# Attention over a key-value cache on one core: the first K block loaded in two transfers, 16 partitions and then 112

## The chip, the core and the metric

The kernel runs on one core of a Trainium2 chip. Its time is the device time of one execution in microseconds. A core has five engines that run side by side, each with its own instruction list: TensorE (PE) for matrix products, VectorE (DVE), ScalarE (ACT), GpSimd (POOL) and SyncE (SP), which here does nothing but issue loads and one store. Loads are carried out by 16 DMA engines. On-chip memory has 128 partitions; a tile is so many partitions by so many bytes in each.

## The reference

Grouped-query attention with four new tokens for each of eight sequences, over a cache of 2048 keys: 32 query heads share 8 key-value heads.

```python
B, Sq, D = 8, 4, 512
Hq, Hkv, Sk, Dh = 32, 8, 2048, 128
q = (x @ wq).reshape(B, Sq, Hq, Dh).transpose(0, 2, 1, 3)
k = repeat(k_cache, Hq // Hkv, axis=1)
v = repeat(v_cache, Hq // Hkv, axis=1)
scores = einsum("bhqd,bhkd->bhqk", q, k) * Dh ** -0.5
p = softmax(scores)
o = einsum("bhqk,bhkd->bhqd", p, v)
out = o.transpose(0, 2, 1, 3).reshape(B, Sq, Hq * Dh) @ wo
```

All tensors are bf16. The two caches hold 33.5 MB each, wq and wo 4.2 MB each: about 75.5 MB must be read.

## The kernel before

The work is cut into 16 units; a unit `u` is four key-value heads of one sequence. Its keys are one tile of 128 partitions with 16 KB in each (2 MB): partition `g * 32 + s` holds 64 consecutive keys of head `g`. The 2 MB are one contiguous piece of the cache. `load_k(u)` loads the keys of a unit with one transfer (lines 88 to 91), `load_v(u)` the values (line 99). Three buffers each stand for K and V.

All loads are issued by SyncE on one queue, in an order written by hand: K0, then `wq_sb` (line 107, 4 MB), `x_sb` (line 108, 32 KB), K1, K2, V0; then K3, V1, K4, V2 and so on, and at last the four blocks of wo in six pieces (line 104). `load_ready` issues a load as soon as its buffer can be free in the program's order; on the chip the issue then waits until the buffer's last reader is done. The queue works through its transfers in the order of issue, 16 DMA engines side by side, and several transfers stand in it at any time.

The steps of a unit:

- `turn_keys` (line 137): VectorE turns the keys in two halves with 32 by 32 transposes, `kt` from `k_sb`. The first of them waits for the K load. When both are done, the K buffer is free and SP can issue the next K load into it.
- `scores` (line 215): TensorE multiplies queries (`q_bd`) and turned keys.
- `maxima`, `exponentials`, `probs_to_keys`: VectorE takes the maximum (line 233), ScalarE the exponential (line 251), VectorE turns the result (line 261), and ScalarE and GpSimd copy it to `probs` (line 271).
- `values` (line 300): TensorE multiplies with V, two units later.

Before unit 0's scores can run, the queries are made: x is turned (line 147, into `xT_sb`, line 150), multiplied with wq (line 157), scaled (lines 172 and 174), turned (line 181) and spread (line 193). All of this needs x, which stands in the queue behind K0 and wq. Unit 0's two transposes come first on VectorE, ahead of the copy of line 150.

At the end TensorE projects with wo (`project`, line 368), ScalarE copies `out_ps` (line 432) and two small stores write the output.

Of the kernel before, what the change touches and what calls it, by code (L numbers as in the profile page):

```python
# [8 lines left out]
BF16 = mybir.dt.bfloat16  # L9
# [5 lines left out]
def kernel(  # L15
# [9 lines left out]
    nc = tc.nc  # L25

    B, Sq, D = x.shape
    _, Hkv, Sk, Dh = k_cache.shape
# [5 lines left out]
    G = 4  # L34
    S = 128 // G
    C = Sk // S
# [18 lines left out]
    kpool = ctx.enter_context(tc.tile_pool(name="kpool", bufs=KB))  # L55
# [25 lines left out]
    units = [(hq, b) for hq in range(Hkv // G) for b in range(B)]  # L81
    ks = [None] * NU
    vs = [None] * NU

    def load_k(u):
        hq, b = units[u]
        ks[u] = kpool.tile([128, C, Dh], BF16, tag="k_sb", name="k_sb")
        nc.sync.dma_start(
            ks[u][:, :, :],
            k_cache[b, G * hq : G * hq + G].rearrange("g (s c) d -> (g s) c d", c=C),  # L90
        )
# [11 lines left out]
        w0 = p * WR + r0  # L103
        nc.sync.dma_start(wo_sb[:, w0 : w0 + n, :], rows[:, r0 : r0 + n, :])

    load_k(0)
    nc.sync.dma_start(wq_sb[:, :, :], wq.rearrange("(p r) n -> p r n", r=R))
    nc.sync.dma_start(x_sb[:, :], x.flatten_outer_dims())
    loads = [("k", 1)]
# [355 lines left out]
```

## Time and profile before

| | |
|---|---|
| three runs | 185.65, 190.73, 190.85 us; median 190.73 |
| the profiled execution | 185.65 us |
| its span, first to last instruction | 183.9 us |
| mean granted TensorE clock | 0.907 |
| busy: PE, DVE, ACT, POOL | 124.5, 119.3, 83.3, 57.2 us |
| read from memory | 75.53 MB, 411 GB/s over the span |
| issue to landing: K0, x, median of K loads | 7.9, 17.0, 20.3 us |

The profile is of one execution. Its page gives the busy time of each engine, then the span in 40 equal slices, where a digit is the busy share of a slice in tenths (9 is 90% or more); the DMA line is the mean over the 16 DMA engines. The chain of waits follows the work that ended last back to what released each step. Times in the timeline are microseconds from the start of the span, with the start first and the duration behind it; what stands in brackets is the idle time before an instruction and what ended it. "SPq" is an issue of a load on SyncE's queue: its duration is that of the issue and not of the transfer.

### The profile page before, as it was taken

Reading aid. Unit: us, or ns where it says so; the run is one execution under the profiler, and the core shown is the slowest. Engines: PE = TensorE matmul, PEld = TensorE weight load, DVE = VectorE, ACT = ScalarE, POOL = GpSimd, SP = SyncE. Lnnn points to the kernel's source line nnn. Section 1 sums busy time; section 2 is a strip of 40 time slices with the busy share of each in tenths; the row PEclk is TensorE's granted clock in tenths of the full one; section 3 lists DMA queues with packets and bytes.
Section 4 is the critical chain, followed back from the end, with each engine's and each line's share of the span. In section 5 each row is a group of like instructions: output and inputs, shape, how many; then the busy total and the mean of one; then the engine's idle time right before and its main releaser. Section 6 shows DMA issues by size and latency. Waiting matters only on the chain.

```text
span 183.9 us, 2569 instructions
## 1 busy us (share of the span) xinstructions
PE 124.5 (68%) x964; PEld 82.1 (45%) x964; DVE 119.3 (65%) x147; ACT 83.3 (45%) x154; POOL 57.2 (31%) x122
## 2 busy tenths in 40 slices
PE   0000465437959796887978858399867977499992
PEld 0000141202626574755736626247453746269770
DVE  0180234968597989989889777567857685936210
ACT  2000130272825674946847646346572638084020
POOL 8920000152405151632534515142332415056000
PEclk9999999655887999999999999958996699879999
DMA  6999999999999999999999999999999999999980
GB/s 185 471 435 389 442 417 446 417 442 428 424 442 417 446 413 437 421 435 431 428 431 428 438 413 438 438 428 435 417 442 417 442 421 435 438 411 429 421 366 19
DMA packets 5915, 75.71 MB, mean 412 GB/s; under 512 B 688, under 2 KB 784, under 8 KB 1296
## 3 DMA queue, kind: packets, MB, share of 16 engines
q1 hardware_dynamic: 5856, 75.55, 96.8%
q8 instruction: 7, 0.11, 0.2%
q14 instruction: 4, 0.03, 0.0%
q10 hardware_dynamic: 48, 0.02, 0.0%
HBM read 75.53 MB, written 0.03 MB: 411 GB/s over the span
## 4 chain that ended last, share of the span: by engine, by line
DMA 51%; DVE 30%; PE 14%; ACT 2%; issue 1%; SPq 0%; ACTq 0%; DVEq 0%
DMA k_sb<-in_k_cache_dram 24%; DVE kt L137 21%; DMA v_sb<-in_v_cache_dram 9%; DMA x_sb<-in_x_dram 9%; PE s_ps L215 9%; DMA wo_sb<-in_wo_dram 8%; DVE top L233 5%; PE o_ps L300 3%; DVE swapped L225 1%; DVE q_g L174 1%; PE psq L157 1%; DVE q_bd L193 1%; ACT q_g L172 1%; PE pse L181 1%; DVE less L239 1%
## 5 line engine op out<-in xcount | busy, mean ns | idle before, releaser
L137 DVE STREAM_TRANSPOSE kt<-k_sb 128x2048 f32<-128x2048 f32 x32 | 72.0, 2288 | 17.5 <-DMA k_sb<-in_k_cache_dram 17.4
L215 PE MATMUL s_ps<-kt,q_bd 128*64 128x512 bf16 x256 | 44.5, 479 | 33.1 <-DVE kt L137 33.1
L300 PE MATMUL o_ps<-v_sb,probs 128*128 128x256 bf16 x512 | 61.3, 281 | 0.0
L271 POOL COPY probs<-p_t 32x512 bf16<-32x512 bf16 x63 | 38.6, 612 | 59.4 <-DVE r_sb L289 57.1
L300 PEld LDWEIGHTS <-probs 128*128 128x128 bf16 x512 | 50.5, 101 | 12.1 <-issue 5.2
L271 ACT COPY probs<-p_t 32x512 bf16<-32x512 bf16 x62 | 38.1, 615 | 19.7 <-DVE r_sb L289 18.5
L215 PEld LDWEIGHTS <-q_bd 128*64 128x64 bf16 x256 | 17.3, 126 | 49.7 <-issue 25.2
L233 DVE TENSOR_REDUCE top<-s_ps 128x1 f32<-128x1024 f32 x16 | 19.6, 1224 | 16.7 <-PE s_ps L215 16.7
L251 ACT ACTIVATE s_sb<-s_ps,less 128x1024 bf16<-128x1024 f32 x16 | 22.4, 1400 | 9.8 <-DVE less L239 9.6
L225 POOL COPY l_swapped<-l_sb 64x1 f32<-64x1 f32 x32 | 5.8, 180 | 50.3 <-ACT s_sb L251 49.6
L324 ACT CAST oT<-o_t 128x64 bf16<-128x64 f32 x16 | 3.4, 212 | 33.3 <-PE o_t L323 33.3
L147 PE MATMUL xtp<-ident,x_sb 32*128 32x32 bf16 x4 | 0.3, 194 | 18.7 <-DMA x_sb<-in_x_dram 18.7
L316 ACT ACTIVATE o_sc<-o_ps,r_sb 64x128 f32<-64x128 f32 x28 | 10.1, 362 | 5.9 <-PE o_ps L300 5.7
L172 ACT ACTIVATE q_g<-psq 32x512 bf16<-32x512 f32 x4 | 2.4, 588 | 21.6 <-DVE q_g L174 21.6
L261 DVE STREAM_TRANSPOSE p_t<-s_sb 128x512 f32<-128x512 f32 x16 | 10.7, 672 | 1.6 <-ACT s_sb L251 1.6
L147 PEld LDWEIGHTS <-x_sb 32*128 32x128 bf16 x4 | 0.2, 114 | 18.7 <-DMA x_sb<-in_x_dram 18.7
L323 PEld LDWEIGHTS o_t<-both,o_sc 128*128 128x128 f32 x32 | 5.4, 211 | 7.1 <-issue 6.1
L323 PE MATMUL o_t<-both,o_sc 128*128 128x64 f32 x32 | 7.5, 320 | 0.2 <-DVE o_sc L318 0.2
L130 POOL MEMSET probs<- 128x4096 bf16 x2 | 7.0, 3511 | 0.0
L174 DVE TENSOR_SCALAR q_g<-psq 32x512 bf16<-32x512 f32 x4 | 2.7, 681 | 4.4 <-ACT q_g L172 2.3
L181 PE MATMUL pse<-ident,q_g 128*128 128x128 bf16 x32 | 3.3, 263 | 3.3 <-ACT q_g L172 2.9
L225 DVE COPY swapped<-top 64x1 f32<-64x1 f32 x32 | 4.7, 148 | 0.8
(32 smaller groups left out, 48.5 us busy)
## 6 DMA issues: line engine op xcount, KB each, us to landing
k_sb<-in_k_cache_dram SPq DMA_DIRECT2D x16, 2048.0 KB, 20.3
v_sb<-in_v_cache_dram SPq DMA_DIRECT2D x15, 2048.0 KB, 19.8
wq_sb<-in_wq_dram SPq DMA_DIRECT2D x1, 4096.0 KB, 17.3
wo_sb<-in_wo_dram SPq DMA_DIRECT2D x3, 1024.0 KB, 18.6
v_sb<-in_v_cache_dram SPq DMA_DIRECT2D x1, 1536.0 KB, 13.8
v_sb<-in_v_cache_dram SPq DMA_DIRECT2D x1, 512.0 KB, 14.6
wo_sb<-in_wo_dram SPq DMA_DIRECT2D x1, 512.0 KB, 21.3
wo_sb<-in_wo_dram SPq DMA_DIRECT2D x2, 256.0 KB, 16.9
```

The costliest lines, as they stand in the source:

```text
L130: nc.gpsimd.memset(pr[:, :, :, :, :, :], 0.0)
L137: nc.vector.transpose(kts[(u, t)][:, :, :, :, :].rearrange("k c h s e -> k (c h s e)").bitcast(FP32), ks[u][:, t * CT : (t + 1) * CT, :].r ...
L181: nc.tensor.matmul(pse[:, h, :, :, :].rearrange("d g b s -> d (g b s)"), lhsT=q_g[:, h, k, e, :, :].rearrange("t g w -> t (g w)"), rhs=ide ...
L215: nc.tensor.matmul(s_pss[u][h * NQ : (h + 1) * NQ, t, :, :], lhsT=q_bd[:, hq, k, e, b, :, :].rearrange("k g q -> k (g q)"), rhs=kts[(u, t) ...
L225: engine.tensor_copy(out=out[h * NQ : (h + 1) * NQ, :], in_=in_[(1 - h) * NQ : (2 - h) * NQ, :])
L233: nc.vector.reduce_max(out=top[:, :], in_=s_pss[u][:, :, :, :].rearrange("q t c s -> q (t c s)"), axis=AX,)
L251: nc.scalar.activation(out=s_sbs[u][:, :, :, :].rearrange("q a s j -> q a j s"), in_=s_pss[u][:, :, :, :].rearrange("q t (a j) s -> q (t a ...
L261: nc.vector.transpose(p_t[:, :, :, :, :].rearrange("s x g q j -> s (x g q j)").bitcast(FP32), s_sbs[u][:, :, :, :].rearrange("q a s j -> q ...
L271: by[h * G + g](out=probs[u % PB][g * S : (g + 1) * S, h, :, :, g, :], in_=p_t[quad * S : (quad + 1) * S, :, g % 2, :, :].rearrange("s x q ...
L300: nc.tensor.matmul(o_pss[u][:, :, :].rearrange("n j d -> n (j d)"), lhsT=probs[u % PB][:, h, t * CT // 4 + a, :, :, :].rearrange("s j g q ...
L316: nc.scalar.mul(out=to, in_=of, mul=by)
L323: nc.tensor.matmul(o_t[:, :], lhsT=o_scs[u][:, :], rhs=both[:, :], start=True, stop=True)
```

## The change

`load_k(0)` is replaced by `load_first_k()`, which loads the same bytes into the same tile with two transfers: partitions 0 to 15 (256 KB), then partitions 16 to 127 (1.75 MB). Both are issued by SyncE, one after the other, ahead of wq. All other loads are as they were.

```diff
-    load_k(0)
+    def load_first_k():
+        hq, b = units[0]
+        ks[0] = kpool.tile([128, C, Dh], BF16, tag="k_sb", name="k_sb")
+        of = k_cache[b, G * hq : G * hq + G].rearrange("g (s c) d -> (g s) c d", c=C)
+        for q0, q1 in ((0, 16), (16, 128)):
+            nc.sync.dma_start(ks[0][q0:q1, :, :], of[q0:q1, :, :])
+
+    load_first_k()
     nc.sync.dma_start(wq_sb[:, :, :], wq.rearrange("(p r) n -> p r n", r=R))
     nc.sync.dma_start(x_sb[:, :], x.flatten_outer_dims())
```

In the built program SyncE's list has one issue more. The first transpose of unit 0 waits for the completions of both transfers, and so does the issue of K3, which reuses the buffer. The order of the instructions on the other engines is the same.

## The prediction

> **What bounds the kernel now.** I read the page's head and its DMA parts first, because a change to a load can only matter where loads matter.
>
> ```profile
> span 183.9 us, 2569 instructions
> ...
> DMA  6999999999999999999999999999999999999980
> GB/s 185 471 435 389 442 417 446 417 442 428 424 442 417 446 413 437 421 435 431 428 431 428 438 413 438 438 428 435 417 442 417 442 421 435 438 411 429 421 366 19
> ...
> q1 hardware_dynamic: 5856, 75.55, 96.8%
> ```
>
> The line DMA is the busy share of the 16 DMA engines in 40 slices of 4.6 us: 9 from the second slice to the last but one. The line q1 says that one queue, SP's, moves 75.55 MB and keeps 16 engines busy for 96.8% of the span. No compute engine comes near that (PE 68%, VectorE 65%). The stage table says the same with less rounding; the columns are the stage, its length, busy time of PE, PEld, DVE, ACT and POOL, the granted clock, the DMA share and GB/s.
>
> ```profile
> 1.77:4.00 2.23, 0.00 (x0) 0.00 (x0) 0.23 (x1) 0.25 (x1) 2.23 (x3) 1.00 1.01 264
> ...
> 40.00:80.00 40.00, 30.99 (x240) 19.97 (x241) 34.25 (x40) 22.93 (x42) 12.44 (x31) 0.87 1.01 429
> 80.00:120.00 40.00, 30.04 (x244) 20.71 (x245) 32.76 (x41) 24.03 (x44) 14.86 (x35) 0.99 1.00 429
> ...
> 178.00:180.20 2.20, 1.78 (x28) 1.21 (x26) 0.00 (x0) 0.00 (x0) 0.00 (x0) 1.00 0.46 178
> ```
>
> Between 40 and 120 us the stream runs at 429 GB/s with a share of 1.00 whatever the clock (0.87 or 0.99). So an engine moves 429 / 16 = 26.8 GB/s, and a partition's 16 KB of a K block takes it 16384 / 26.8 = 0.61 us. Only at the two ends is the stream slower: 264 GB/s just after it starts, and 178 in the last two microseconds, when some engines are done and others not. The last wait in the chain of waits closes the argument:
>
> ```profile
> 165.40 14.73 DMA wo_sb<-in_wo_dram
> 180.13 0.04 issue
> 180.17 0.41 PE out_ps L368 x4
> 180.58 0.02 issue
> 180.60 0.36 ACT out_sb L432
> ```
>
> The kernel ends 3.7 us after the last piece of wo lands at 180.13, and it lands when the slowest DMA engine has come to the end of its list. All loads stand on one queue with equal shares for the 16 engines, and these never rest; a microsecond that an engine loses anywhere is not made up. Whatever the edit costs the slowest engine moves the end by as much.
>
> **The change, part by part.** These are the SP queue's first issues, from the timeline.
>
> ```profile
> 0.74 0.37 SPq L88 DMA_DIRECT2D k_sb<-in_k_cache_dram  x1
> 1.16 0.42 SPq L107 DMA_DIRECT2D wq_sb<-in_wq_dram  x1
> 1.63 0.42 SPq L108 DMA_DIRECT2D x_sb<-in_x_dram  x1
> ...
> 2.10 1.10 SPq L88 DMA_DIRECT2D k_sb<-in_k_cache_dram  x2
> 3.24 0.47 SPq L99 DMA_DIRECT2D v_sb<-in_v_cache_dram  x1
> ...
> 8.62 4.50 DVE L137 STREAM_TRANSPOSE kt<-k_sb 128x2048 f32<-128x2048 f32 x2 [6.54 <-DMA k_sb<-in_k_cache_dram]
> 13.15 0.33 SPq L88 DMA_DIRECT2D k_sb<-in_k_cache_dram  x1
> ```
>
> *One more issue.* An issue takes 0.33 to 0.47 us; wq, x, K1, K2 and V0 are each issued some 0.42 us later. Cost nothing: wq at 1.58 instead of 1.16 stands behind 2 MB of K0 that keep the engines busy until about 8 us. Without that cover it would be the 0.42.
>
> *The hand-over from 16 to 112 partitions.* The first packet moves at 1.77, 0.66 us after the first issue ends at 1.11. The second issue would end near 1.55 and its packets be ready near 2.2. The first packets cannot be through by 1.77 + 0.61 = 2.38. So no engine runs dry: nothing. If the cover failed: 0.42.
>
> *Waits.* The first transpose of L137 and the fourth K issue on SP now wait for two completions instead of one. Behind the transposes on VectorE stands the copy of xT_sb, which waits for x until 18.65 anyway, 5.5 us after the transposes end at 13.12. Behind the fourth K issue (13.15) stand V1 and K4. By then 4 MB of wq and three 2 MB blocks are still queued, which last beyond 30 us. So K0 may land several microseconds later, and neither wait costs anything. One completion per engine more is far under 0.1 us.
>
> *How the rows meet the engines.* Here is the price. A K row of 16 KB lies in one partition and arrives at 26.8 GB/s, so one partition is not the limit. But 16 × 26.8 GB/s can belong to the engines, or equally to 16 paths into the memory, each serving eight partitions, one row at a time. All large loads of the trace cover 128 partitions, where the two can't be told apart. Nor does x help (32 partitions, 1 KB each): its packets are spread over 17.2 to 18.0 us, too thin to meet one another.
>
> For the first transfer, sixteen rows start at once into 16 neighbouring partitions. If these lie on 16 paths, it takes 0.61 us as now: +0. On 8 paths 1.22 (+0.61), on 4 paths 2.44 (+1.83), on 2 paths, if paths hold neighbours only, 8 × 0.61 = 4.89 (+4.28). No row is nearer to one of the four, so I take their mean, (0 + 0.61 + 1.83 + 4.28) / 4 = 1.7 us.
>
> For the second transfer, an engine has seven rows instead of eight, 7 × 0.61 = 4.28 us. 112 partitions do not divide into one group of eight for each engine; two engines will at times want one path. Never: +0. Always in pairs: +4.28. I take half, 2.1.
>
> The sum: 1.7 + 2.1 = 3.8 us more on the slowest engine, none of it hidden. The profiled execution took 185.65 us, of which its span is 183.9 and 1.75 lie around it. 185.65 + 3.8 = 189.45, rounded 189.5, 2.1% more. The bounds of the sum are 0 and 8.6 (185.65 and 194.2). The median of the three runs shown, 190.73, lies 5.08 above the profiled execution, which is their fastest; the sum stands against the fastest, and a result is to be set beside runs like it.
>
> [...]
>
> **The rivals.**
>
> *The rate is the engines' own, and the start gets tidier (the other side).* Place: the stage 1.77 to 4.00. At 264 GB/s in place of 429 it loses 2.23 × (1 − 264 / 429) = 0.86 us, because engines begin one after another and first packets are slow. A shorter first transfer may put a row before each engine sooner, and would then return up to 0.86: 184.8, half of it 185.2. It decides if the first sixteen rows take less than about 1.2 us. For it: the share of 1.01 already there says that engines were busy, not short of lists, and busy engines are what the page would show under either theory. Against it: a slow first access would stay slow for the smaller transfer. Chance 0.17.
>
> *The queue runs dry at the hand-over.* The second list arrives a whole issue and a start late, 0.42 + 0.66 = 1.1: 186.7. Against: the packets ahead last longer than that, worked out above. Chance 0.05.
>
> *The engines march together.* If the seven rounds of the second transfer each put sixteen rows into sixteen neighbouring partitions, each pays what the first pays, 8 × 1.7 = 13.6: 199.3. Against: neighbouring rows to one engine would keep engines seven partitions apart. Chance 0.06.
>
> *Faster by more than 2%.* Two of three runs took 5.1 us more than the third, and the page doesn't show why. If the start of the stream decides which it is, a changed start could bring the short one each time: 185.65 against 190.73, 2.7% less. Nothing in the page speaks for it. Chance 0.05.
>
> *The transfer is hidden anyway, or the change does nothing.* K0 is indeed needed late: its scores wait for q until 26.5. But its bytes occupy the queue, and that is where the price lies. The order of SP's instructions holds two transfers, of 16 and 112 rows, in place of one, so the change does what it says; its chance is within the first rival's.
>
> **How the numbers follow.** The forecast's mechanism, a loss between 0.9 and 8.6 us, has 0.67. About 2% (3.7 us) is what a measurement of this kernel can tell from no change. The sum lies on that line, and more room is above it than below (3.7 to 8.6, against 0.9 to 3.7): 0.44 above, 0.23 below. Slower: 0.44 + 0.06 = 0.50. Within: 0.23 + 0.17 + 0.05 = 0.45. Faster: 0.05. The range goes from 185.0, most of the tidier start, to the upper bound of the sum, 194.3; outside it are the marching engines, the big gain and the tail of the small one, some 0.15. The forecast alone spans 186.5 to 194.2.
>
> **What would show it.** Right: the first sixteen 16 KB rows take about 2.3 us, some packets between 2 and 9 us last well over 0.61; K0's transposes start near 12.4 instead of 8.62, x lands near 22.4 instead of 18.65; from there all is the old trace shifted, 429 GB/s between 40 and 120 us, the last wo near 183.9. Wrong: transposes at 8.6 or earlier (the engines' own rate); a hole in the DMA share at 2 to 3 us (dry queue); a late x but an end that is not late (slack which I deny); or a mid-stream rate under 429 (then the spread of the engines disturbs more than the start).

## The result, and the profile after

Six executions of the changed kernel have a median of 188.9 us (188.61 to 193.82), six of the kernel before 189.88 (185.56 to 191.98). These medians can't be set side by side: some executions of both kernels take 3 to 6 us longer than the others (a profile under cols8 shows such a one, with a stretch of some 46 us at 387 GB/s instead of 429), and the ratios, and the times that stand beside one another from here on, are of the shorter ones. The ratio is 1.0166, 95% interval [1.0153, 1.0179]: from about 185.6 to about 188.7, 3.1 us slower. The profiled execution took 189.11, 3.46 more than the profiled one of before; the three other short ones took 188.61 to 188.69.

The page of the changed kernel, the lines that answer to those of before:

```profile
span 187.3 us, 2571 instructions
...
DMA  6999999999999999999999999999999999999990
GB/s 112 280 392 441 381 430 430 441 416 430 444 413 434 437 436 416 434 436 415 430 437 427 434 430 434 423 434 430 420 441 430 434 430 423 434 416 425 423 368 24
...
q1 hardware_dynamic: 5872, 75.55, 96.9%
```

The engines are as busy as before, in the second slice too, but move 280 GB/s there instead of 471. They are not short of work; their rows take longer (after the first sixteen, K0's rows of 16 KB take 1.72 and then 0.97 us, 0.80 and 0.61 before). The stage table of the changed kernel (stage, length, busy time of PE, PEld, DVE, ACT, POOL, clock, DMA share, GB/s; a packet counts, with its whole time and size, where it starts, so that a share can lie above 1):

```profile
1.77:4.00 2.23, 0.00 (x0) 0.00 (x0) 0.23 (x1) 0.24 (x1) 2.23 (x3) 1.00 1.37 228
4.00:8.00 4.00, 0.00 (x0) 0.00 (x0) 0.00 (x0) 0.00 (x0) 4.00 (x2) 1.00 0.92 254
8.00:12.00 4.00, 0.00 (x0) 0.00 (x0) 0.00 (x0) 0.00 (x0) 2.47 (x1) 1.00 0.94 270
...
40.00:80.00 40.00, 31.13 (x232) 19.51 (x229) 32.57 (x41) 23.87 (x42) 14.25 (x32) 0.80 1.01 430
```

and two of these stages before:

```profile
4.00:8.00 4.00, 0.00 (x0) 0.00 (x0) 0.00 (x0) 0.00 (x0) 4.00 (x2) 1.00 1.12 479
8.00:12.00 4.00, 0.00 (x0) 0.00 (x0) 3.38 (x2) 0.00 (x0) 2.47 (x1) 1.00 0.97 418
```

Nearly all of the loss lies between 4 and 12 us (a little, 228 against 264, before 4); in mid-stream the rate is what it was, 430 against 429. The timeline shows what is late by it; the last line is that of before:

```profile
0.74 0.85 SPq L111 DMA_DIRECT2D k_sb<-in_k_cache_dram  x2
...
1.64 0.42 SPq L114 DMA_DIRECT2D wq_sb<-in_wq_dram  x1
...
12.19 4.50 DVE L144 STREAM_TRANSPOSE kt<-k_sb 128x2048 f32<-128x2048 f32 x2 [10.11 <-DMA k_sb<-in_k_cache_dram]
16.72 0.33 SPq L88 DMA_DIRECT2D k_sb<-in_k_cache_dram  x1
...
21.96 0.32 PE L154 MATMUL xtp<-ident,x_sb 32*128 32x32 bf16 x4 [21.96 <-DMA x_sb<-in_x_dram]
```

```profile
18.70 0.31 PE L147 MATMUL xtp<-ident,x_sb 32*128 32x32 bf16 x4 [18.70 <-DMA x_sb<-in_x_dram]
```

K0's transposes start 3.57 us later (8.62 before), x is used 3.26 later (18.70 before). At the other end the chain of waits reads as before, shifted:

```profile
168.86 14.78 DMA wo_sb<-in_wo_dram
183.64 0.04 issue
183.68 0.41 PE out_ps L375 x4
```

The last wo lands 3.51 us later (180.13 before). What the queue lost at its start is still missing at its end.

### The profile page after: what moved, and what is told of

Same layout as the page of the kernel before. It is cut to its first block, busy times and chain, and to the rows that moved or that the text cites. A ratio compares the mean times of both kernels' runs of the same rounds, so it can differ in the third digit from the quotient of the medians.

```text
span 187.3 us, 2571 instructions
## 1 busy us (share of the span) xinstructions
PE 124.8 (67%) x964; PEld 82.2 (44%) x964; DVE 119.3 (64%) x147; ACT 83.3 (44%) x154; POOL 57.2 (31%) x122
## 4 chain that ended last, share of the span: by engine, by line
DMA 53%; DVE 29%; PE 13%; ACT 2%; issue 1%; SPq 1%; ACTq 0%; DVEq 0%
DMA k_sb<-in_k_cache_dram 24%; DVE kt L144 20%; DMA v_sb<-in_v_cache_dram 11%; DMA x_sb<-in_x_dram 11%; PE s_ps L222 8%; DMA wo_sb<-in_wo_dram 8%; DVE top L240 5%; PE o_ps L307 2%; DVE swapped L232 1%; DVE q_g L181 1%; PE psq L164 1%; DVE q_bd L200 1%; ACT q_g L179 1%; PE pse L188 1%; DVE less L246 1%
## 5 line engine op out<-in xcount | busy, mean ns | idle before, releaser
L258 ACT ACTIVATE s_sb<-s_ps,less 128x1024 bf16<-128x1024 f32 x16 | 22.4, 1401 | 10.0 <-DVE less L246 9.8
L375 PE MATMUL out_ps<-wo_sb,oP 128*32 128x256 bf16 x64 | 4.9, 274 | 1.0 <-DMA wo_sb<-in_wo_dram 0.9
```

What stands on the lines that cost most here:

```text
L258: nc.scalar.activation(out=s_sbs[u][:, :, :, :].rearrange("q a s j -> q a j s"), in_=s_pss[u][:, :, :, :].rearrange("q t (a j) s -> q (t a ...
```

## The experiments

The theories: A, several DMA engines share one write path when a transfer covers 16 or 112 partitions; B, a further transfer costs by itself; C, it is a matter of the start; D, the addresses read matter. Later ones stand in the expectations. Times and ratios are against the kernel before in the same session (185.6 to 186.3).

**cols8: the same two sizes, cut along the keys.**

```diff
-        for q0, q1 in ((0, 16), (16, 128)):
-            nc.sync.dma_start(ks[0][q0:q1, :, :], of[q0:q1, :, :])
+        for c0, c1 in ((0, 8), (8, 64)):
+            nc.sync.dma_start(ks[0][:, c0:c1, :], of[:, c0:c1, :])
```

> K0 is still loaded in two transfers of the same sizes (256 KB and 1.75 MB), but cut along the keys of each partition: all 128 partitions take 2 KB each, then 14 KB each. Theory A (the rows of a 16- or 112-partition transfer make several DMA engines write over one path into the memory): all paths are used evenly, so no loss: within 0.5 us of the kernel before (185.1 to 186.2 in its fast condition), x lands near 18.7. Theory B (a second transfer costs by itself, by its issue and its hand-over): as slow as the changed kernel, some 3 us more (188.7), x near 22. Theory C (the first, small transfer is what starts slowly): also some 3 us more.

Four executions took 190.55 to 194.09, a ratio of 1.0311 if they are set against the kernel before as they are. The profile says that this is not the cut. Two lines of the timeline, and the page's GB/s in 40 slices:

```profile
8.76 4.50 DVE L144 STREAM_TRANSPOSE kt<-k_sb 128x2048 f32<-128x2048 f32 x2 [6.69 <-DMA k_sb<-in_k_cache_dram]
...
18.65 0.31 PE L154 MATMUL xtp<-ident,x_sb 32*128 32x32 bf16 x4 [18.65 <-DMA x_sb<-in_x_dram]
```

```profile
GB/s 195 464 437 382 403 382 389 385 389 385 389 385 389 389 415 437 429 432 420 437 427 434 431 427 431 431 437 427 427 427 437 427 434 427 431 424 419 421 371 20
```

K0 and x arrive as in the kernel before (0.14 later and 0.05 earlier). Then, from about 20 to 66 us, the fifth to the fourteenth slice, the stream runs at 387 GB/s instead of 429, and behind it at 429 again. That stretch of some 46 us costs 46 × (1 − 387 / 429) = 4.5 us, nearly the whole difference of 4.8. The same kernel without it:

> The same kernel as cols8 (K0 as 2 KB and then 14 KB in each of 128 partitions). In cols8's profile K0's transposes began at 8.76 and x was used at 18.65, as in the kernel before, and then rows took 681 instead of 611 ns from about 18 to 64 us. Theory A: the 681 ns stretch has nothing to do with the cut; executions without it are within 0.5 us of the kernel before (185.1 to 186.2). Theory G: this cut brings the stretch on, so all executions stay at 190 to 192.

Two of six executions took 186.16 and 186.26, and the profile of the second has no such stretch (423 to 441 GB/s in the fifth to the fourteenth slice); ratio 1.0015 [0.9976, 1.0054]. Theories B and C fall, and so does G: a second transfer and a small first one cost nothing that shows (at most 0.5%) if all 128 partitions take part.

**flat8: the same addresses read, written across 128 partitions.**

```diff
+        flat = k_cache[b, G * hq : G * hq + G].rearrange("g s d -> (g s d)")
+        for c0, c1 in ((0, 8), (8, 64)):
+            piece = flat[128 * c0 * Dh : 128 * c1 * Dh]
+            nc.sync.dma_start(
+                ks[0][:, c0:c1, :], piece.rearrange("(p c d) -> p c d", p=128, d=Dh)
+            )
```

> The first transfer reads the same contiguous 256 KB as in the changed kernel and the second the same contiguous 1.75 MB, but each is written across all 128 partitions, 2 KB and then 14 KB in each. The keys of unit 0 so stand in another order, and unit 0's part of the output is not the reference's. Theory A (write paths): no loss, within 0.5 us of the kernel before (185.1 to 186.2). Theory D (the addresses read: 16 engines reading neighbouring 16 KB, then pieces 112 KB apart, meet in the DRAM): the loss stays, about 3 us (188.7).

One execution of four can be compared, 185.69.

> The same kernel as flat8 (the addresses of the changed kernel's two transfers, each written across all 128 partitions; unit 0's keys in another order, so that its part of the output is not the reference's). Theory A (write paths): 185.1 to 186.2 in the fast executions. Theory D (addresses read): about 188.7.

Five of six: 185.35 to 185.58, ratio 0.9975 [0.9957, 0.9993]. The two pieces of memory are read here without a loss, if in runs of 2 and 14 KB in place of 16 (310, 474 and 393 GB/s in the stages 1.77 to 4, 4 to 8 and 8 to 12 us of flat8_again, 264, 479 and 418 before: 4.2 MB in both), so D falls too: the loss is on the side that is written. (The quarter per cent is no version to keep: this order mixes the heads in a partition.)

**half64, quarter32, eight16, eight16s: K0 in 2, 4 and 8 transfers.**

```diff
-        for q0, q1 in ((0, 16), (16, 128)):
+        for q0, q1 in ((0, 64), (64, 128)):                        # half64
+        for q0, q1 in ((0, 32), (32, 64), (64, 96), (96, 128)):    # quarter32
+        for q0, q1 in ((0, 16), (16, 32), ..., (112, 128)):        # eight16
             nc.sync.dma_start(ks[0][q0:q1, :, :], of[q0:q1, :, :])
+        for j in range(8):                                         # eight16s
+            nc.sync.dma_start(ks[0][j:128:8, :, :], of[j:128:8, :, :])
```

> K0 in two transfers of 64 partitions, 0 to 63 and 64 to 127. Each engine has four rows in each. Theory A with eight paths behind 64 partitions: the engines go in pairs on one path, each 16 KB row takes 1.22 instead of 0.61 us, 8 rows 9.8 instead of 4.9: 4.9 us more, less what the slow start hides, 4 to 5: 189.6 to 190.6, more than the changed kernel. Theories B, C and D give no reason for more than the changed kernel's 3 us (188.7); if paths held 64 partitions as well as 128, no loss (185.6).

> The same kernel as half64 (K0 as partitions 0 to 63 and 64 to 127). Theory A with eight paths behind 64 partitions: rows of K0 take 1.2 to 1.3 us, K0's transposes start about 4.3 later than before, x lands some 5 later, and the end moves by 4 to 5: 189.6 to 190.6. Theories B, C and D: 188.7 at most.

> K0 in four transfers of 32 partitions. Theory A with eight paths behind 32 partitions as behind 64: as half64, a row takes 1.2 to 1.3 us, 4 to 5 us more: 189.6 to 190.6. Theory P (a transfer's rate goes by the number of its partitions: 64 half, 32 a quarter): a row takes 2.4 us, eight of them 19.6 instead of 4.9: some 14 us more, about 200.

> K0 in eight transfers of 16 neighbouring partitions. Theory A with four paths behind 16 neighbours: rows of 2.4 us while all engines are in one transfer; engines that get ahead work in the next sixteen partitions, partly on other paths, so less than 8 x 1.83 = 14.6 us: 8 to 13 more, 193.6 to 198.6. Theory P (rate by the number of partitions): 16 partitions at an eighth of the rate, 8 x 4.3 = 34 us more, 220. Theory B (a price for each transfer more, 3 us each): 7 x 3 = 21 us more, 207.

> K0 in eight transfers of 16 partitions as eight16, but each takes every eighth partition (j, j+8, ..., j+120). Theory A: every eighth partition reaches eight paths instead of four, so rows take 1.2 to 1.3 us: 4 to 6 us more, 189.6 to 191.6, clearly less than eight16. Theories P and B: the same as eight16.

| K0 in | time, us | more than before | transposes of K0 start |
|---|---|---|---|
| 1 x 128 | 185.6 to 186.3 | | 8.62 |
| 2 x 64 | 190.17 and, run again, 190.22 | 4.5 | 13.15 |
| 4 x 32 | 190.32 | 4.6 | 13.16 |
| 8 x 16, neighbours | 197.18 to 197.53 | 11.5, ratio 1.0621 [1.0605, 1.0637] | 20.89 |
| 8 x 16, every eighth | 189.79 | 4.0 | 13.16 |

The times of half64, quarter32 and eight16s are of one execution in each run and have no interval; the three starts in the table agree to 0.01 us (the other profile of half64 has 13.08). The stages 4 to 8 and 8 to 12 us of half64_again, eight16 and eight16s, in this order:

```profile
4.00:8.00 4.00, 0.00 (x0) 0.00 (x0) 0.00 (x0) 0.00 (x0) 4.00 (x2) 1.00 1.09 229
8.00:12.00 4.00, 0.00 (x0) 0.00 (x0) 0.00 (x0) 0.00 (x0) 2.47 (x1) 1.00 1.11 254
```

```profile
4.00:8.00 4.00, 0.00 (x0) 0.00 (x0) 0.00 (x0) 0.00 (x0) 4.00 (x2) 1.00 0.87 102
8.00:12.00 4.00, 0.00 (x0) 0.00 (x0) 0.00 (x0) 0.00 (x0) 2.48 (x1) 1.00 0.94 111
```

```profile
4.00:8.00 4.00, 0.00 (x0) 0.00 (x0) 0.00 (x0) 0.00 (x0) 4.00 (x2) 1.00 1.04 221
8.00:12.00 4.00, 0.00 (x0) 0.00 (x0) 0.00 (x0) 0.00 (x0) 2.48 (x1) 1.00 1.13 266
```

102 to 111 GB/s is about a quarter of 429 (107), 221 and 229 are about a half (214), and in all three the engines' share is 0.87 to 1.13: they are busy, and their rows take longer. (The 254 and 266 hold the first rows of wq, from 11.54 us on.) The packets of the traces say the same without edges of stages: the 96 rows of 16 KB that start from 4.87 to 17.15 us in eight16 take 2.20 us each, 3.6 times 0.61; the middle rows of half64_again, quarter32 and eight16s take 1.24 to 1.26, twice 0.61.

Sixteen neighbours run at a little over a quarter, sixteen partitions eight apart at a half, though count, sizes and number of transfers are the same; 32 neighbours run like 64 (225 GB/s between 4 and 8 us in quarter32, 229 in half64_again). So P falls (a rate by the number of partitions), and B once more. What counts in these runs is which partitions are written together. How many paths stand behind them no run shows: four behind sixteen neighbours and eight behind the other three are the author's reading of these rates. That eight16 takes 3.6 and not 4 times as long fits its expectation, by which engines that are ahead write into the next sixteen partitions; no run shows that by itself.

**mid4, mid1, midcols: the cut in mid-stream.** K0 stays whole.

```diff
-        nc.sync.dma_start(ks[u][:, :, :], k_cache[...])
+        cuts = [0, 16, 128] if u in (4, 6, 8, 10) else [0, 128]    # mid4; mid1: u == 8
+        for q0, q1 in zip(cuts, cuts[1:]):
+            nc.sync.dma_start(ks[u][q0:q1, :, :], of[q0:q1, :, :])
+        cuts = [0, 8, 64] if u == 8 else [0, 64]                   # midcols
+        for c0, c1 in zip(cuts, cuts[1:]):
+            nc.sync.dma_start(ks[u][:, c0:c1, :], of[:, c0:c1, :])
```

> K0 is loaded whole again; instead the K blocks of units 4, 6, 8 and 10 are loaded as 16 and then 112 partitions, in the middle of the full stream. Theory A: each split costs what it cost at the start or more, as no slow start hides the first transfer: 3 to 5 us each, 12 to 20 in all: 198 to 206. Theory C (a matter of the start): nothing, 185.6. Theory E (the loss at the start is there because the queue has slack to lose before the first scores, mid-stream splits being absorbed by the full queue): nothing, 185.6.

213.12 and 215.02 (two of four executions); ratio 1.1525 [1.1451, 1.1598], 28 us more, 7 for each split. C and E fall (no matter of the start, and the full queue absorbed none of these 28 us), but A's 12 to 20 was too small.

> Only the K block of unit 8 is loaded as 16 and then 112 partitions, about 55 us into the stream; K0 is whole. Theory A (several engines on one write path): the first sixteen rows take about 2.4 us each (sixteen engines on four paths) and the next seven about 1 us each; the sum over one engine is 1.8 + 2 to 3 us, and engines that fall out of step meet others' rows in the block behind it, so 4 to 7 us more: 189.6 to 192.6 (the four splits of mid4 cost 28 together, 7 each). Theory F (a split costs its 3 us wherever it stands and mid4's surplus came from the four splits disturbing one another): 188.6.

192.75 to 193.22; ratio 1.038 [1.0346, 1.0414], 7.1 us for the one split, just above A's 4 to 7. Four times that is 28: the splits of mid4 add up, and F falls. The block is written some 80 us into the stream (the expectation says 55). The stage table of mid1, and its packets between 81.1 and 81.9 us:

```profile
75.00:80.00 5.00, 3.73 (x30) 2.24 (x29) 4.49 (x5) 2.50 (x7) 1.66 (x5) 1.00 1.02 433
80.00:85.00 5.00, 4.27 (x36) 3.02 (x35) 4.92 (x6) 3.57 (x7) 1.86 (x6) 1.00 1.09 180
85.00:90.00 5.00, 4.00 (x35) 3.05 (x35) 2.85 (x7) 3.85 (x7) 2.42 (x4) 1.00 1.00 249
90.00:95.00 5.00, 0.74 (x7) 0.42 (x5) 0.00 (x0) 0.84 (x4) 0.55 (x3) 0.78 0.93 239
95.00:100.00 5.00, 2.17 (x10) 0.86 (x10) 4.54 (x3) 0.00 (x0) 0.00 (x0) 0.50 1.01 433
```

```profile
DMA packets 14, 0.11 MB, mean 143 GB/s; under 512 B 7, under 2 KB 7, under 8 KB 7
...
q1 hardware_dynamic: 14, 0.11, 141.5%
```

The three slow stages lose 5 × (249 + 180 + 190) = 3.1 MB against 429 GB/s, 3.1 MB / 429 GB/s = 7.2 us: the whole price. Of the 14 packets in the narrow stage seven are completions of a few bytes; the other seven, rows of 16 KB, took 1.415 × 16 × 0.8 / 7 = 2.6 us each, near the 2.44 that theory A with four paths estimates (4 × 0.61). The slow rows are more than the block has: of the 203 rows of 16 KB that start from 80 to 95 us 187 took over 0.66 us, and the block has 128, so at least 59 belong to the blocks beside it. What the 203 took beyond 0.61, added up and shared among 16 engines, is 7.2 us again.

> Only the K block of unit 8 is cut, as in mid1, but along the keys: 2 KB and then 14 KB in each of 128 partitions. Theory A: no loss, within 0.5 us of the kernel before (185.1 to 186.2), the stream stays at 429 GB/s around 80 us. Theory B (a second transfer in mid-stream costs by itself): about 193, as mid1.

185.72 and 185.81 (two of four executions), ratio 0.9998 [0.9978, 1.0018]. The profiled execution, 192.84, is a longer one, and its cut block comes later than that of mid1: the two transfers, issued from 72.44 on, land 18.0 and 21.9 us after their issues, at about 90 and 95. The stages before that:

```profile
85.00:90.00 5.00, 2.29 (x14) 1.33 (x16) 5.00 (x4) 0.63 (x3) 0.19 (x1) 0.81 1.00 416
90.00:95.00 5.00, 5.00 (x26) 2.93 (x23) 2.00 (x7) 3.90 (x6) 2.51 (x5) 0.50 1.03 442
```

Their mean is 429 GB/s. So the cut costs nothing that shows in mid-stream either, if it leaves 128 partitions.

## Why the prediction was right or wrong, point by point

- *The queue binds, and nothing it loses is made up*: right. K0, x and the last wo are late by 3.57, 3.26 and 3.51 us, and the end by 3.46. The times named as signs came: 12.19 for 12.4, 21.96 for 22.4, 183.64 for 183.9.
- *The extra issue, the hand-over and the waits cost nothing*: right. wq is issued 0.48 later (1.64 against 1.16), the fourth K load 3.57 later, and neither shows. cols8_again has the same extra issue and the same double waits at a ratio of 1.0015.
- *The mechanism, paths into the memory shared by several engines*: the runs fit it. eight16 against eight16s, with the same number and sizes of transfers, shows that the partitions written set the rate (2.20 against 1.24 to 1.26 us for a row). The paths themselves, that there are 16 of them and that each serves eight partitions are a supposition of the forecast that no run shows. The addresses that a transfer reads differ between the two as well, but the addresses of the changed kernel cost nothing in flat8_again.
- *The size*: the forecast was 3.8 us over an execution like the profiled one, 189.5; measured 3.1 (2.8 to 3.3 by the interval), about 188.7. The direction held, the sum was 0.7 too large (0.3 between the two profiled executions). It lay just beyond 2% and the result, 1.66%, just within; the chances had slower (0.50) ahead of within (0.45), the wrong way round.
- *The step that failed* is "none of it hidden", in the first term. The term counts the first sixteen rows from 0.61 us, the time of a row in mid-stream. The packets of the two traces, in order of start, sixteen rows (on average one for each engine) at a time, show what K0's rows took:

| rows of K0 | before, mean us | changed, mean us | more for an engine |
|---|---|---|---|
| first 16 | 1.34 | 1.38 | 0.04 |
| second 16 | 0.80 | 1.72 | 0.92 |
| the other 96, six for an engine | 0.61 | 0.97 | 2.17 |

The first group of before, in the window from 1.76 to 2.805 us, and the three of the changed kernel, in windows from 1.76 to 2.06, 2.58 to 3.72 and 4.71 to 10.17 (the second with the 16 completions of the first transfer, a few bytes each):

```profile
q1 hardware_dynamic: 16, 0.26, 128.4%
```

```profile
q1 hardware_dynamic: 16, 0.26, 459.9%
...
q1 hardware_dynamic: 32, 0.26, 154.4%
...
q1 hardware_dynamic: 96, 1.57, 107.1%
```

The first row takes 1.284 × 16 × 1.045 / 16 = 1.34 us before and 4.599 × 16 × 0.30 / 16 = 1.38 after; the last group 1.071 × 16 × 5.46 / 96 = 0.97. So a first row took 1.34 us before the change too, 0.73 more than in mid-stream. Four paths are the number that comes nearest to eight16 (2.20 us for a row, estimated 2.44), and their estimate of 1.83 less these 0.73 is 1.10; measured are 0.04 + 0.92 = 0.96 over the two rows in which the first transfer can be felt, where the sum has 1.7. The prediction had priced the slow start, at 0.86, as a rival, and did not set it against the term. (That 1.7, a mean over four possible numbers of paths, lay near the 1.83 of four is luck.)
- *Where the first transfer's wait is seen*: its rows were expected to take 2.3 us and took 1.38. The issue list shows when the two transfers land:

```profile
k_sb<-in_k_cache_dram SPq DMA_DIRECT2D x1, 1792.0 KB, 10.9
k_sb<-in_k_cache_dram SPq DMA_DIRECT2D x1, 256.0 KB, 4.4
```

The first lands 4.4 us after its issue, at 5.1, though its last row ends at 3.70 in the records. So here the record of a packet ended 1.4 us before the transfer counted as landed. That the wait stands in the engine's next row, a row of the second transfer, is the author's reading; the 1.72 us of those rows fit it.
- *The second term*, 2.1, half of 4.28, was a middle between bounds, and near: the six rows of an engine that start from 4.7 us on, as the first transfer lands, cost 2.17 more. Besides, wq's 128 rows behind them took 1.255 us each in place of 1.213, 0.34 for an engine, which the sum does not have. Together: 0.96 + 2.17 + 0.34 = 3.47, the 3.46 between the profiled executions.
- *In mid-stream* the same cut costs 7.1, and the sum has 3.8. The sum counts the block's own rows alone, and there at least 59 rows of other blocks are slow with them. The 256 KB transfer of mid1, issued at 70.71, lands 16.7 us later by the issue list, at 87.4, 6.7 us after the rate falls at 80.75 (481 GB/s in the 0.375 us before, 218 in the 0.375 us behind); in the changed kernel the first transfer lands 3.4 us after its first packet. This fits engines that reach the sixteen rows far apart in mid-stream, and within 0.3 us (1.77 to 2.05) at the start. That this is why the start is cheaper is argued and not shown.
- *The rivals*: the tidier start (184.8 to 186.1) did not come; cols8_again and flat8_again, which start with a small transfer into all 128 partitions, are within 0.3% of the kernel before. The dry queue did not show: the first row ends at 2.59, and a row of the second transfer starts in the same 0.01 us. The engines marching together is what eight16 sets up, for 11.5 us and not 13.6. A gain over 2% did not come: 193.3 and 193.8 occur with the change too.
- *The base*: the sum stands against 185.65 and not against the median of 190.73. That was the right choice: against that median 188.7 reads as a gain where there is a loss.
- *Readings that were off and change nothing*: the last slice but one of the DMA line is an 8 and not a 9; an issue took up to 0.61 us and not 0.47; and at 13.15 us 4.7 MB had started, so some 1.6 MB of wq and not 4 MB was still queued, which with the three K and V blocks still lasts to about 31 us.

## What to carry to other kernels

In a kernel whose loads keep the queue full (here 96.8% of the span), count for each transfer which partitions it writes: cut a load along the bytes of a partition (ratios 1.0015 at the start and 0.9998 in mid-stream) and not across partitions (3.1 to 11.5 us for one 2 MB block), so that every transfer covers all 128. A load that is needed late is not free to be slow; it costs its time in the queue and delays all that stands behind it (K0 3.57 us later, the end 3.46). A smaller first transfer brought no earlier start here in either form (K0's transposes at 12.19 and 8.76, 8.62 before).

## What the runs showed of the hardware that was not expected

- The stretch: in the profile of cols8 rows of 16 KB take 681 instead of 611 ns (387 against 429 GB/s) from some 20 to 66 us; 810 of the 848 rows that start between 24 and 60 us are slow, so it is no matter of a few engines. flat8_again shows the same in nearly the same place (376 GB/s from 20 to 60 us, 431 before). The profiled executions of flat8, half64 and midcols are longer too than the shortest of the same kernels (190.32, 197.81 and 192.84 us against 185.69, 190.17 and 185.72). What brings it on is open, and so is why single executions of cols8_again (215.61) and half64 (206.57), without a profile, took far longer still.
- A 16 KB row's record was hardly longer (1.38 us, 1.34 before) in the very transfer into sixteen neighbouring partitions, and long (1.72, 0.80 before) in the transfer behind it.
- One 2 MB block cut at partition 16 in mid-stream costs 7.1 us, more than the 4.9 us that the block takes whole; the same cut at the start of the stream costs 3.1.
